# Attention and feed-forward on one core: values' products with tokens on partitions from the third block on, and one burst for values and the next scores in the main loop

## The chip, the cores and the metric

The kernel runs on one core of a Trainium2 chip. The metric is the device time of one execution in microseconds; 0.2% of it, 1.2 us, is about what a measurement of this kernel can tell from no change.

## The reference, cut to what matters

Local attention over chunks of 32 tokens (each chunk sees 8 memory keys, 16 tokens to its left, itself and 8 tokens to its right, so 64 keys), and on its result two large products with a smooth gate between them. Everything is float32.

```python
B, H, S, D = 4, 8, 768, 64                      # 3072 tokens, 24 chunks of 32 per sequence
for c in range(nc):                             # per chunk
    k_full = np.concatenate([mem_k, k_ctx], axis=2)      # 64 keys
    v_full = np.concatenate([mem_v, v_ctx], axis=2)
    scores = scale * np.matmul(q_c, k_full.transpose(0, 1, 3, 2))
    a = np.exp(scores - np.max(scores, axis=-1, keepdims=True))
    a = a / (np.sum(a, axis=-1, keepdims=True) + 1e-09)
    out[:, :, c_start:c_end] = np.matmul(a, v_full)      # "values' products"
x = out.transpose(0, 2, 1, 3).reshape(B * S, H * D)      # 3072 x 512
h = x @ w_in                                             # 512 x 2048
g = np.where(h >= 1, h, np.where(h <= -1, 0.0, (h + 1) ** 2 / 4))
return g @ w_out                                         # 2048 x 512
```

## The kernel before

The 3072 tokens are six blocks (NB) of 512. A block's attention is done in two halves of 256 tokens, a half being one key `(block, half)` in the code. The feed-forward of a block is 16 steps: step `s` makes 128 of the 2048 hidden features for all 512 tokens (`pe_hidden`, 12 matmuls of 128x128 by 512 into one PSUM bank of the pool `ps_h`, which has two), passes them through the gate on ScalarE and VectorE (`gating`, `gate_sum`, `gate_high`, `gate_low`), and multiplies them with `w_out` (`pe_out`, 12 matmuls into the block's accumulators `ps_o`). Twelve, since each float32 operand is split in a high and a low part of TensorE's faster type (`xth`/`xtl`, `gh`/`gl`, two parts of the weights `wr`), and three of the four products are made. LAG = 2: at step `s` TensorE does `pe_hidden(s)` and then `pe_out(s-2)`, so two steps pass between a hidden feature and its use.

A half's attention is a chain of stages. `pe_scores` makes 64 products of 32 query tokens with 64 keys into the two-bank PSUM tile "s"; the products are float32 and small, eight places of the array (64 rows by 32 columns) hold one each. Each is done by two instruction pairs, so a burst is 128 weight loads and 128 matmuls in the profile. `less_max` and `normalise` make the softmax on VectorE with the exponential on ScalarE; `transpose_prob` turns the probabilities on VectorE in 32x32 squares (six STREAM_TRANSPOSE, `pt<-pr`). `pe_values` takes the values as the stationary operand (64 keys by 64 features, four places of the array) and the turned probabilities as the moving one (32 tokens), so that the result has features on partitions, as `pe_hidden` wants x. It too is 64 products, 128 pairs, into the tile "s" again, now named `ps_x`. `x_high` (ScalarE) and `x_low` (VectorE) split that result into `xth` and `xtl`.

The order of the work is the program's: every engine call goes through the wrapper `InOrder`, whose line, 63, is the line of nearly all rows of the profile. The first third of the program is ordered by the hand-written string `FIRST` (blocks 0 and 1 of the feed-forward, attention of blocks 0 to 2; the names n2 and n3 in it are the halves of block 2). From there on the loop over `s` from step 32 to 95 sets it: blocks 2 to 5 of the feed-forward, and the attention of blocks 3 to 5, six halves, ahead of their use. `STARTS = (3, 9)` puts the scores of the halves at steps 3 and 9 of each of the three blocks before; the next three steps hold softmax, transposes and values, so that the values' burst comes three steps after the scores' (`begin.get(s - stage)`). In a step, TensorE's order is: scores or values burst if there is one, `pe_hidden(s)`, `pe_out(s-2)`. Each burst therefore stands by itself between the large matmuls. The loads of the next half (`load_qk`, 1.5 MB, and `load_v`, 1 MB, one buffer each) are issued by SyncE when the burst that used the buffer is done.

Of the kernel before, what the change touches and what calls it, by code (L numbers as in the profile page):

```python
# [8 lines left out]
F32 = mybir.dt.float32  # L9
# [13 lines left out]
LAG = 2  # L23


STARTS = (3, 9)

# [13 lines left out]
    w15 J13 J15 n1 J15 n1 J14 C0 J15 n1 J14 n1 n1 C0 n1 n1 J15 C1 n1 n1 J15 n1 C1 n1 n1 C1 C0 C1 C2  # L43
    J15 J15 C0 C1 n1 J15 J15 C0 C2 C2 C0 + n1 C2 n1 n1 C3 C2 C1 C3 C3 D0 C3 C3 C2 D0 D0 D1 D0 D0 n2
    D1 D1 D2 D1 + n2 C3 D1 D2 n2 D0 D2 n2 D2 D3 n2 D2 D1 n2 n2 D3 n2 E4 D3 n2 D3 n2 n2 n2 D2 E4 D3
    n2 E5 n2 E4 E4 E4 D3 E5 E6 E5 E5 E5 E4 E6 E6 E6 n2 E6 E7 + n2 n2 n2 n3 E7 E5 + n3 n3 E7 E8 n3 E7
    n3 n3 n3 E6 n3 E8 n3 n3 n3 E9 n3 n3 n3 E8 n3 E7 E8 E9 E8 E7 + n3 E9 E9 n3 n3 E9 E10 E8 E10 E10
    E10 E11 E10 E9 E11 E11 E11 E12 E11 E10 E12 E12 E12 E13 E12 E11 E13 E13 E13 E14 E13 E12 E14 E14
    E14 E15 E14 E13 E15 E15 E15 E15
"""  # L50

LAST = 2
# [16 lines left out]
def attn_ffn_kernel(ctx: ExitStack, tc: tile.TileContext, first_qk, first_v, qk, vw, w, out):  # L69
# [51 lines left out]
    def load_qk(blk, half):  # L121
        t = qk_of[blk, half] = apool.tile([P, NP, QKN], F32, name="qk", tag="qk")
        sp.dma_start(t, qk[blk - 1, half].rearrange("p (h f) -> p h f", h=NP))

    def load_v(blk, half):
        t = v_of[blk, half] = apool.tile([P, NP, VN], F32, name="v", tag="v")
        sp.dma_start(t, vw[blk - 1, half].rearrange("p (h f) -> p h f", h=NP))
# [40 lines left out]
        yield  # L168


    scores_of, prob, prob_t, banks, xts, both = {}, {}, {}, {}, {}, {}

    def x_of(blk):
        if blk not in xts:
# [113 lines left out]
    def pe_scores(key):  # L288
        src = qk_of.pop(key)
        ps = scores_of[key] = two_banks("s", "ps_s")  # L290
        s = ps.rearrange("p h (r t w) -> p h r t w", r=NP, w=W)
        for r in range(NP):
            for c in range(HC):
                t, j = divmod(c, P // CHUNK)
                for h in range(2):
                    rows, k0 = slice(h * D, (h + 1) * D), HT + c * W
                    pe.matmul(
                        s[j * CHUNK : (j + 1) * CHUNK, h, r, t],
                        src[rows, r, c * CHUNK : (c + 1) * CHUNK],
                        src[rows, r, k0 : k0 + W],  # L300
                        start=True,
                        stop=True,
                    )
# [24 lines left out]
    def pe_values(key):  # L328

        ps = banks[key] = two_banks("s", "ps_x")  # L330
        o = ps.rearrange("p a (r t b q) -> p a r t b q", r=NP, t=2, q=CHUNK)
        pt = prob_t.pop(key).rearrange("p b (h r t) q -> p b h r t q", h=2, r=NP)
        v = v_of.pop(key).rearrange("p r (t b h d) -> p r t b h d", t=2, b=2, h=2)
        for r in range(NP):
            for t in range(2):
                for b in range(2):
                    for a in range(2):
                        rows = slice(a * D, (a + 1) * D)
                        for h in range(2):
                            pe.matmul(  # L340
                                o[h * D : (h + 1) * D, a, r, t, b],
                                v[rows, r, t, b, h],
                                pt[rows, b, h, r, t],
                                start=True,
                                stop=True,
                            )
# [10 lines left out]
    def x_high(key):  # L357
        for a in range(2):
            src, hi, _ = x_views(key, a)
            act.copy(hi, src)  # L360

    def x_low(key):
        for a in range(2):
            src, hi, lo = x_views(key, a)
            dve.tensor_tensor(lo, src, hi.bitcast(F32), op=ALU.subtract)
            yield
        banks.pop(key)

    def attention(key):

        pe_scores(key)
        yield
        yield from less_max(key)
        act.activation(prob[key], prob[key], AF.Exp, scale=SCALE)
        yield
        yield from normalise(prob[key])
        yield from transpose_prob(key)
        pe_values(key)
        yield
        x_high(key)  # L380
        yield
        yield from x_low(key)

    def run(*chains):

# [174 lines left out]
        next(chains[name])  # L560


    begin = {}
    first = 2
    for blk in range(first + 1, NB):
        for half in range(2):
            begin[(blk - 1) * NFC + STARTS[half]] = (blk, half)

    def after(key):
        blk, half = key  # L570
        return (blk + half, 1 - half)

    steps = NB * NFC
    for s in range(first * NFC, steps):
        k_scores, k_probs, k_trans, k_values = (begin.get(s - stage) for stage in range(4))
        if k_scores is not None:
            pe_scores(k_scores)
            if after(k_scores)[0] < NB:
                load_qk(*after(k_scores))
        if k_values is not None:  # L580
            pe_values(k_values)
            x_high(k_values)
            if after(k_values)[0] < NB:
                load_v(*after(k_values))
        if s > first * NFC:
            gate_sum(s - 1)
            gate_high(s - 1)
        run(
            gate_low(s - 1) if s > first * NFC else None,
            x_low(k_values) if k_values is not None else None,  # L590
        )
        run(
            less_max(k_scores) if k_scores is not None else None,
            normalise(prob[k_probs]) if k_probs is not None else None,
            transpose_prob(k_trans) if k_trans is not None else None,
        )
        if k_scores is not None:
            act.activation(prob[k_scores], prob[k_scores], AF.Exp, scale=SCALE)
        pe_hidden(s)
        gating(s)  # L600
        if s - LAG >= first * NFC:
            pe_out(s - LAG)
            if (s - LAG) % NFC == NFC - 1:
                store((s - LAG) // NFC)
        else:
            n, i = LAST // LAG, s - first * NFC
            for name in items[len(items) - LAST :][i * n : (i + 1) * n]:
                for _ in chains[name]:
                    pass
    gate_sum(steps - 1)  # L610
    gate_high(steps - 1)
    run(gate_low(steps - 1))
# [16 lines left out]
def _lay_out(q, k, v, mem_k, mem_v, moe_w_in, moe_w_out):  # L629
    import numpy as _np  # L630

    B, H, S, D = q.shape
    NM, NC = mem_k.shape[2], S // CHUNK
    NP, W = H // 2, NM + LEFT + CHUNK + RIGHT
    NB = B * S // TB

    def windows(mem, a):

        pad = _np.pad(a, ((0, 0), (0, 0), (LEFT, RIGHT), (0, 0)))
        win = [  # L640
            _np.concatenate([mem, pad[:, :, c * CHUNK : (c + 1) * CHUNK + LEFT + RIGHT]], axis=2)
            for c in range(NC)
        ]
        return _np.stack(win, axis=1).reshape(B * NC, H, W, D)

    def transposed(a):

        return a.transpose(1, 3, 0, 2).reshape(NP, 2 * D, -1)


    qt = transposed(q).reshape(NP, 2 * D, NB * 2, TB // 2).transpose(2, 1, 0, 3)
    kw = windows(mem_k, k).reshape(NB * 2, NCH // 4, 2, NP, 2, 2, W // 2, D)

    k0 = kw.transpose(0, 4, 7, 3, 1, 2, 5, 6).reshape(NB * 2, 2 * D, NP, NCH // 2 * W)
    kw = _np.stack([kw[:, :, 0], kw[:, :, 1][..., ::-1, :, :]], axis=2)
    kw = kw.transpose(0, 4, 7, 3, 1, 2, 5, 6).reshape(NB * 2, 2 * D, NP, NCH // 2 * W)
    qk0 = _np.concatenate([qt, k0], axis=3)[0:2].reshape(2, 2 * D, 2, -1).transpose(0, 2, 1, 3)
    qk = _np.concatenate([qt, kw], axis=3).reshape(NB, 2, 2 * D, -1)[1:]
    vw = windows(mem_v, v).reshape(NB, NT, 4, NP, 2, W, D)

    v0 = vw[0].reshape(2, 2, 4, NP // 2, 2, 2, W, D).transpose(0, 3, 1, 6, 4, 2, 5, 7)

    v1 = vw[1:].reshape(NB - 1, 2, NT // 2, 2, 2, NP, 2, W, D).transpose(0, 1, 3, 7, 5, 2, 4, 6, 8)
    DM, DF = moe_w_in.shape
    n = DF // 128

    slices = (
        moe_w_in.reshape(DM // 128, 128, n, 128).transpose(2, 1, 0, 3).reshape(n, 128, DM),
        moe_w_out.reshape(n, 128, DM),
    )  # L670
    w = _np.stack([slices[which][fc] for which, fc in weight_order(n)])
    w = w.reshape(n, 2, 128, DM).transpose(0, 2, 1, 3).reshape(n, 128, 2 * DM)
    arrays = {

        "first_qk": qk0.reshape(NP, 2 * D, -1),
        "first_v": v0.reshape(NP, 2 * W, NCH * D),
        "qk": qk,
        "vw": v1.reshape(NB - 1, 2, 2 * W, -1),
        "w": _np.ascontiguousarray(w).view(_np.int64),
    }  # L680
    return {name: _np.ascontiguousarray(a) for name, a in arrays.items()}
# [23 lines left out]
```

## Time and profile before

| what | value |
|---|---|
| median of 3 runs | 600.14 us (599.96 to 600.18) |
| the profiled execution | 600.11 us |
| its span in the trace | 598.3 us |
| TensorE matmuls busy (PE) | 582.7 us, 97% |
| VectorE (DVE) / ScalarE (ACT) busy | 325.6 us, 54% / 280.3 us, 47% |
| chain that ended last | PE 82%, DVE 15%, issue 2%, DMA 1% |

The span is what the profiler sees of the program; 1.8 us of the execution lie outside it. The chain is the work that ended last, followed back from the end: it says which engine set the time at each moment. DVE's share of it lies in the first 107 us, where weights are decoded; from there to the last stores it consists of PE's matmuls alone.

### The profile page before, as it was taken

What the parts mean: (1) busy time and instruction counts of PE and PEld (TensorE: products, weight loads), DVE (VectorE), ACT (ScalarE), POOL (GpSimd) and SP (SyncE); (2) the same over time, 40 slices, a digit from 0 to 9 for tenths busy, and PEclk for the clock granted to TensorE, in tenths of its full rate; (3) what the DMA queues carried; (4) which work ended last, traced back from release to release, by engine and by line L of the source; (5) the groups of instructions that cost most, each with busy time, mean ns of one, the idle gap of its engine ahead of it and who ended that gap; (6) DMA issues with size and microseconds to landing.
All of it is one profiled execution on the core that took longest, in us unless ns stands there. A gap on an engine that the chain in (4) does not pass through costs nothing.

```text
span 598.3 us, 12265 instructions
## 1 busy us (share of the span) xinstructions
PE 582.7 (97%) x5496; PEld 483.5 (81%) x5496; DVE 325.6 (54%) x466; ACT 280.3 (47%) x503; POOL 0.7 (0%) x6
## 2 busy tenths in 40 slices
PE   5899999999999999999999999999999999999996
PEld 2888888788888888888888888888888888888885
DVE  5999999986474224636423644623564632322222
ACT  2689864554435335444435443434443444543442
POOL 0000000000000000000000000000000000000000
PEclk9999999999999999999999999999999999999999
DMA  8999300424051004012101223200310000100001
GB/s 355 422 418 419 148 1 0 178 82 168 1 177 71 0 1 158 26 65 108 71 1 71 107 71 107 71 1 34 144 71 2 1 2 0 71 0 1 0 1 70
DMA packets 9844, 55.31 MB, mean 92 GB/s; under 512 B 1088, under 2 KB 1088, under 8 KB 5184
## 3 DMA queue, kind: packets, MB, share of 16 engines
q1 hardware_dynamic: 9792, 54.53, 23.6%
q8 instruction: 43, 0.70, 0.5%
q14 instruction: 9, 0.07, 0.0%
HBM read 48.23 MB, written 6.29 MB: 91 GB/s over the span
## 4 chain that ended last, share of the span: by engine, by line
PE 82%; DVE 15%; issue 2%; DMA 1%; ACT 0%; DVEq 0%; ACTq 0%
PE ps_o L63 38%; PE ps_h L63 38%; DVE f L63 6%; PE ps_x L63 3%; DVE wr L63 2%; PE ps_s L63 2%; DVE gw L63 1%; DVE gl L63 1%; DVE pr L63 1%; DVE den L63 1%; DMA qk<-in_first_qk_dram 1%; DVE pt L63 1%; DVE mx L63 1%; DVE xtl L63 0%; DVE rin L63 0%
## 5 line engine op out<-in xcount | busy, mean ns | idle before, releaser
L63 PE MATMUL ps_h<-xth,wr 128*128 128x512 f32 (+1 forms) x832 | 195.6, 377 | 1.1 <-DVE wr L63 1.1
L63 PE MATMUL ps_o<-wr,gh 128*128 128x512 f32 x768 | 194.7, 390 | 0.0
L63 PEld LDWEIGHTS ps_h<-xth,wr 128*128 128x128 f32 x832 | 149.0, 190 | 30.3 <-DVE wr L63 1.5
L63 PEld LDWEIGHTS ps_o<-wr,gh 128*128 128x128 f32 x768 | 143.3, 188 | 29.4
L63 DVE SCALAR_TENSOR_TENSOR gw<-gw,gt 128x512 f32<-128x512 f32 (+1 forms) x104 | 67.2, 649 | 164.9 <-ACT gw L63 164.6
L63 ACT ACTIVATE gw<-ps_h 128x512 f32<-128x512 f32 (+1 forms) x104 | 58.6, 563 | 159.0 <-PE ps_h L63 158.9
L63 PE MATMUL ps_o<-wr,gl 128*128 128x512 f32 x384 | 106.9, 389 | 0.0
L63 PE MATMUL ps_h<-xtl,wr 128*128 128x512 f32 (+1 forms) x416 | 104.8, 374 | 0.0
L63 DVE TENSOR_TENSOR gl<-gw,gh 128x512 fp32r<-128x512 f32 (+1 forms) x104 | 67.4, 649 | 65.8 <-ACT gh L63 65.7
L63 ACT CAST gh<-gw 128x512 fp32r<-128x512 f32 (+1 forms) x104 | 61.1, 590 | 69.9 <-DVE gw L63 69.9
L63 PEld LDWEIGHTS ps_h<-xtl,wr 128*128 128x128 f32 x416 | 75.3, 190 | 13.9
L63 PEld LDWEIGHTS ps_o<-wr,gl 128*128 128x128 f32 x384 | 72.1, 188 | 15.1
L63 ACT ACTIVATE gw<-gw 128x512 f32<-128x512 f32 (+1 forms) x104 | 62.4, 600 | 0.0
L63 ACT ACTIVATE gt<-ps_h 128x512 f32<-128x512 f32 (+1 forms) x104 | 58.3, 561 | 0.0
L63 DVE STREAM_TRANSPOSE pt<-pr 32x512 f32<-32x512 f32 (+1 forms) x60 | 41.2, 698 | 1.3
L63 DVE SCALAR_TENSOR_TENSOR f<-w,f 128x1024 uint32<-128x1024 uint32 x32 | 39.0, 1220 | 0.4
L63 ACT ACTIVATE pr<-pr 128x1024 f32<-128x1024 f32 (+1 forms) x14 | 13.1, 937 | 35.1 <-DVE pr L63 35.0
L63 PEld LDWEIGHTS ps_x<-pt,v 64*64 64x64 f32 x1536 | 25.1, 142 | 5.0 <-issue 3.3
L63 PE MATMUL ps_x<-pt,v 64*64 64x32 f32 x1536 | 26.6, 226 | 1.2 <-ACT pt L63 1.2
L63 ACT CAST xth<-ps_x 128x512 fp32r<-128x512 f32 x24 | 13.1, 591 | 20.6 <-PE ps_x L63 20.6
L63 ACT CAST wr<-f 128x1024 fp32r<-128x1024 f32 x16 | 16.8, 1051 | 11.7 <-DVE f L63 11.7
L63 PEld LDWEIGHTS ps_s<-qk 64*32 64x32 f32 x1536 | 17.1, 112 | 6.1 <-issue 3.1
(27 smaller groups left out, 182.6 us busy)
## 6 DMA issues: line engine op xcount, KB each, us to landing
w<-in_w_dram SPq DMA_DIRECT2D x16, 1024.0 KB, 19.8
qk<-in_qk_dram SPq DMA_DIRECT2D x10, 1536.0 KB, 6.5
v<-in_vw_dram SPq DMA_DIRECT2D x10, 1024.0 KB, 5.5
out_dram<-ob SPq DMA_DIRECT2D x24, 256.0 KB, 2.0
qk<-in_first_qk_dram SPq DMA_DIRECT2D x4, 768.0 KB, 8.7
v<-in_first_v_dram SPq DMA_DIRECT2D x4, 512.0 KB, 12.7
```

What stands on the lines that cost most here:

```text
L63: return self.tc.keep_in_program_order(getattr(self.engine, name)(*args, **kwargs))
```

## The change

From block 2 on (`first = 2`) the values' products are made the other way round. `pe_rows` takes the turned probabilities as the stationary operand (64 keys by 32 tokens) and the values as the moving one (64 features), so that tokens are on partitions and the array holds eight products at a time; it is again 64 products, 128 pairs. Since `pe_hidden` needs features on partitions, the result must be turned: `rows_out` copies it from PSUM to the tile `xr` (two ScalarE copies), `turn_rows` turns it on VectorE in six STREAM_TRANSPOSE into the tile `xt`, `split_high` makes `xth` (one ScalarE cast) and `split_low` makes `xtl` (one VectorE subtraction). On the host the second half of each value row is rolled by 32 features, so that quarters of the partitions land where they should.

For the two halves of block 2 (n2 and n3 in `FIRST`) the result stays in the tile "s". In the main loop it goes to the two banks of `ps_h`, the pool of the hidden features, and the schedule changes: `BURSTS = (1, 6, 11, 19, 27, 35, 43)` are seven steps, counted from the loop's first. At the n-th of them the values of half n-1 and the scores of half n follow each other on TensorE without anything between; the first has scores only, the last values only. In a step with values, `pe_out(s-2)` now comes ahead of `pe_hidden(s)`. Softmax and transposes of a half follow its scores one, two and three steps later; the exponential comes behind the gate's three instructions on ScalarE instead of ahead of them. In `FIRST`, n3 starts some steps later than before, with its scores in the place behind n2's values that they had.

The core of the diff:

```diff
-STARTS = (3, 9)
+BURSTS = (1, 6, 11, 19, 27, 35, 43)
+    def pe_rows(key, outs):
+        banks[key] = outs
+        pt = prob_t.pop(key).rearrange("p b (h r t) q -> p b h r t q", h=2, r=NP)
+        v = v_of.pop(key).rearrange("p r (t b h d) -> p r t b h d", t=2, b=2, h=2)
+        for r in range(NP):
+            for t in range(2):
+                for b in range(2):
+                    for a in range(2):
+                        rows = slice(a * D, (a + 1) * D)
+                        for h in range(2):
+                            to, c0 = (2 * h + b) * CHUNK, (r * 2 + t) * D
+                            pe.matmul(
+                                outs[a][to : to + CHUNK, c0 : c0 + D],
+                                pt[rows, b, h, r, t],
+                                v[rows, r, t, b, h],
+                                start=True,
+                                stop=True,
+                            )
+    def rows_out(key):
+        xr = rows_of[key] = apool.tile([P, NP, 2, 2, D], F32, name="xr", tag="pt")
+        for a, src in enumerate(banks.pop(key)):
+            act.copy(xr[:, :, :, a], src.rearrange("p (r t d) -> p r t d", r=NP, t=2))
+    def turn_rows(key):
+        src = rows_of.pop(key).rearrange("p r t a (s q) -> p r (t a) s q", s=2)
+        xt = turned[key] = apool.tile([P, NP, HT], F32, name="xt", tag="pr")
+        dst = xt.rearrange("p r (n b q) -> p r n b q", b=2, q=CHUNK)
+        for b in range(2):
+            dve.transpose(dst[:, :, :, b], src[:, :, :, 0])
+            yield
+        for b in range(2):
+            for h in range(2):
+                of, to = (2 * h + b) * CHUNK, (2 * h + 1 - b) * CHUNK
+                dve.transpose(dst[to : to + CHUNK, :, :, b], src[of : of + CHUNK, :, :, 1])
+                yield
+    def split_high(key):
+        act.copy(x_half(x_of(key[0])[0], key[1]), turned[key])
+    def split_low(key):
+        hi, lo = (x_half(x, key[1]) for x in x_of(key[0]))
+        dve.tensor_tensor(lo, turned.pop(key), hi.bitcast(F32), op=ALU.subtract)
+        yield
...
+    for s in range(first * NFC, steps):
+        stages = [begin.get(s - stage, (None, None)) for stage in range(4)]
+        k_values, k_scores = stages[0]
+        if k_values is not None:
+            pe_rows(k_values, [ps_h.tile([P, 512], F32, name="ps_h") for _ in range(2)])
+            if after(k_values)[0] < NB:
+                load_v(*after(k_values))
+        if k_scores is not None:
+            pe_scores(k_scores)
+            if after(k_scores)[0] < NB:
+                load_qk(*after(k_scores))
+        if k_values is not None:
+            product(s)
+        if s > first * NFC:
+            gate_sum(s - 1)
+            gate_high(s - 1)
+        if k_values is not None:
+            rows_out(k_values)
+        split, k_max = stages[1]
+        run(
+            split_low(split) if split is not None else None,
+            gate_low(s - 1) if s > first * NFC else None,
+        )
...
+        pe_hidden(s)
+        gating(s)
+        if k_values is not None:
+            split_high(k_values)
+        if k_max is not None:
+            act.activation(prob[k_max], prob[k_max], AF.Exp, scale=SCALE)
+        if k_values is None:
+            product(s)
```

TensorE in the main loop, at the seventh step of block 2's feed-forward. Before, this is the values' burst of half (3, 0); `wr_721` and its neighbours are weight tiles, `ps_h<-xth,wr` a hidden group, `ps_o<-wr,gh` an output group, x8 and x4 are counts:

```order
L63 MATMUL ps_h<-xth,wr_721 128x512 x8
L63 MATMUL ps_h<-xtl,wr_721 128x512 x4
L63 MATMUL ps_o<-wr_721,gh 128x512 x8
L63 MATMUL ps_o<-wr_721,gl 128x512 x4
L63 MATMUL ps_x<-pt,v 64x32 x64
L63 MATMUL ps_h<-xth,wr_796 128x512 x8
L63 MATMUL ps_h<-xtl,wr_796 128x512 x4
L63 MATMUL ps_o<-wr_796,gh 128x512 x8
L63 MATMUL ps_o<-wr_796,gl 128x512 x4
```

The same place in the changed kernel, TensorE again:

```order
L63 MATMUL ps_h<-xth,wr_721 128x512 x8
L63 MATMUL ps_h<-xtl,wr_721 128x512 x4
L63 MATMUL ps_o<-wr_721,gh 128x512 x8
L63 MATMUL ps_o<-wr_721,gl 128x512 x4
L63 MATMUL ps_h<-v,pt 32x64 x64
L63 MATMUL ps_s<-qk 32x64 x64
L63 MATMUL ps_o<-wr_796,gh 128x512 x8
L63 MATMUL ps_o<-wr_796,gl 128x512 x4
L63 MATMUL ps_h<-xth,wr_796 128x512 x8
L63 MATMUL ps_h<-xtl,wr_796 128x512 x4
L63 MATMUL ps_h<-xth,wr_850 128x512 x8
L63 MATMUL ps_h<-xtl,wr_850 128x512 x4
```

The scores of the next half have moved up behind the values, the values are written by tiles of the scores' form, and the output group of this step stands ahead of its hidden group, so that two hidden groups follow each other.

VectorE around the same values' burst, before:

```order
L63 SCALAR_TENSOR_TENSOR gw<-gw,gt 128x512
L63 TENSOR_TENSOR gl<-gw,gh 128x512
L63 TENSOR_TENSOR xtl<-ps_x,xth 128x4x2x64 x2
L63 SCALAR_TENSOR_TENSOR gw<-gw,gt 128x512
L63 TENSOR_TENSOR gl<-gw,gh 128x512
```

VectorE around it in the changed kernel:

```order
L63 SCALAR_TENSOR_TENSOR gw<-gw,gt 128x512
L63 TENSOR_TENSOR gl<-gw,gh 128x512
L63 STREAM_TRANSPOSE xt<-xr 128x16x32 x2
L63 STREAM_TRANSPOSE xt<-xr 32x16x32 x4
L63 SCALAR_TENSOR_TENSOR gw<-gw,gt 128x512
L63 TENSOR_TENSOR xtl<-xt,xth 128x4x256
L63 TENSOR_TENSOR gl<-gw,gh 128x512
L63 MEMSET ps_s 32x8x8
L63 TENSOR_REDUCE mx<-ps_s 128x16
L63 TENSOR_TENSOR pr<-ps_s,mx 128x1024
```

Six transposes stand behind the gate of the step before, and the subtraction and the next half's softmax follow in the step after it.

ScalarE around the burst in the changed kernel (before, two casts `xth<-ps_x` stood ahead of a `gh<-gw`):

```order
L63 CAST gh<-gw 128x512
L63 COPY xr<-ps_h 128x8x64 x2
L63 ACTIVATE gw<-ps_h 128x512
L63 ACTIVATE gt<-ps_h 128x512
L63 ACTIVATE gw<-gw 128x512
L63 CAST xth<-xt 128x4x256
L63 CAST gh<-gw 128x512
```

The copies out of PSUM stand behind `gh` of the step before, and the cast to `xth` stands ahead of `gh` of the burst's own step.

## Rows read from the trace of the kernel before

**Rows 1.** Busy time in the main loop: us, then each engine, PEclk, DMA share, GB/s.

```profile
222.23:585.50 363.27, 363.27 (x3037) 300.25 (x3037) 155.61 (x224) 153.63 (x275) 0.00 (x0) 1.00 0.14 49
```

**Rows 2.** Chain that ended last, main loop: start us, us, what.

```profile
233.11 1.41 PE ps_s L63 x91
234.52 2.97 PE ps_h L63 x12
237.49 2.72 PE ps_o L63 x12
...
251.09 2.00 PE ps_x L63 x128
253.09 2.95 PE ps_h L63 x12
```

**Rows 3.** Timeline of PE, main loop: start us, us, instruction, count.

```profile
232.04 1.07 PE L63 MATMUL ps_o<-wr,gl 128*128 128x512 f32 x4
233.04 1.48 PE L63 MATMUL ps_s<-qk 64*32 64x64 f32 x128
234.45 2.12 PE L63 MATMUL ps_h<-xth,wr 128*128 128x512 f32 x8
236.41 1.08 PE L63 MATMUL ps_h<-xtl,wr 128*128 128x512 f32 x4
...
239.14 1.07 PE L63 MATMUL ps_o<-wr,gl 128*128 128x512 f32 x4
240.04 1.98 PE L63 MATMUL ps_h<-xth,wr 128*128 128x512 f32 x8
241.86 1.07 PE L63 MATMUL ps_h<-xtl,wr 128*128 128x512 f32 x4
...
251.02 2.07 PE L63 MATMUL ps_x<-pt,v 64*64 64x32 f32 x128
253.01 2.11 PE L63 MATMUL ps_h<-xth,wr 128*128 128x512 f32 x8
```

**Rows 4.** Groups by form, whole span: count, busy us, mean ns, idle before.

```profile
L63 PE MATMUL ps_x<-pt,v 64*64 64x32 f32 x1536 | 26.6, 226 | 1.2 <-ACT pt L63 1.2
L63 PE MATMUL ps_s<-qk 64*32 64x64 f32 x1536 | 19.6, 239 | 1.1 <-DMA qk<-in_first_qk_dram 1.1
```

**Rows 5.** The same chain at the halves of block 2 (n2, n3).

```profile
161.71 2.00 PE ps_x L63 x128
163.71 2.95 PE ps_h L63 x12
...
179.20 2.00 PE ps_x L63 x128
```

**Rows 6.** Waits of PEld from 160 us on: total us, times, longest.

```profile
PEld ps_x L63 <- issue: 2.8, 8, 0.4
PEld ps_s L63 <- issue: 2.5, 7, 0.4
```

**Rows 7.** Groups by form, VectorE and ScalarE, whole span.

```profile
L63 DVE STREAM_TRANSPOSE pt<-pr 32x512 f32<-32x512 f32 x40 | 28.1, 703 | 1.2
L63 DVE TENSOR_TENSOR wr<-f,wr 128x1024 fp32r<-128x1024 f32 x16 | 19.5, 1218 | 0.0
L63 ACT CAST wr<-f 128x1024 fp32r<-128x1024 f32 x16 | 16.8, 1051 | 11.7 <-DVE f L63 11.7
L63 DVE TENSOR_TENSOR xtl<-ps_x,xth 128x512 fp32r<-128x512 f32 x24 | 15.6, 684 | 3.0 <-ACT xth L63 3.0
L63 DVE STREAM_TRANSPOSE pt<-pr 128x512 f32<-128x512 f32 x20 | 13.1, 689 | 0.1
L63 ACT CAST xth<-ps_x 128x512 fp32r<-128x512 f32 x24 | 13.1, 591 | 20.6 <-PE ps_x L63 20.6
```

**Rows 8.** Timeline of DVE and ACT just ahead of a burst.

```profile
251.03 0.69 DVE L63 SCALAR_TENSOR_TENSOR gw<-gw,gt 128x512 f32<-128x512 f32 x1
...
248.90 0.59 ACT L63 ACTIVATE gt<-ps_h 128x512 f32<-128x512 f32 x1
249.38 0.63 ACT L63 ACTIVATE gw<-gw 128x512 f32<-128x512 f32 x1
```

**Rows 9.** DMA issues: count, KB each, median us to landing.

```profile
qk<-in_qk_dram SPq DMA_DIRECT2D x10, 1536.0 KB, 6.5
```

More of the change, by code (lines that the diff above doesn't have):

```diff
@@ L45 @@
     D1 D1 D2 D1 + n2 C3 D1 D2 n2 D0 D2 n2 D2 D3 n2 D2 D1 n2 n2 D3 n2 E4 D3 n2 D3 n2 n2 n2 D2 E4 D3
[L46 to L49, printed above, removed]
+    n2 E5 n2 E4 E4 E4 D3 E5 E6 E5 E5 E5 E4 E6 E6 E6 n2 E6 E7 + n2 n2 n2 E7 n3 E5 + n2 n2 E7 E8 E7 n2
+    E7 n2 E6 n2 E8 n2 n3 E8 E9 E8 n3 E8 E7 n3 E9 n3 E9 n3 n3 n3 E10 E9 E9 E8 E10 n3 n3 E10 n3 E11
+    E10 E10 n3 E9 E11 n3 n3 E11 E12 E11 E11 E10 n3 + E12 n3 E12 n3 n3 E13 E12 E12 n3 E11 E13 n3 n3
+    E13 E14 E13 E13 n3 E12 n3 E14 n3 E14 E15 E14 E14 E13 E15 E15 E15 E15
 """
@@ L168, in decode @@
         yield
-    scores_of, prob, prob_t, banks, xts, both = {}, {}, {}, {}, {}, {}
+    scores_of, prob, prob_t, banks, rows_of, turned, xts, both = {}, {}, {}, {}, {}, {}, {}, {}
+    first = 2
     def x_of(blk):
@@ L367, in x_low, with x_half @@
         banks.pop(key)
+    def pe_rows(key, outs):
[20 more added lines that the diff above has]
+            act.copy(xr[:, :, :, a], src.rearrange("p (r t d) -> p r t d", r=NP, t=2))
+    def x_half(x, half):
+        return x[:, :, half * HT : (half + 1) * HT]
+    def turn_rows(key):
[16 more added lines that the diff above has]
+        yield
     def attention(key):
@@ L377, in attention @@
         yield from transpose_prob(key)
-        pe_values(key)
+        if key[0] < first:
+            pe_values(key)
+            yield
+            x_high(key)
+            yield
+            yield from x_low(key)
+            return
+        ps = two_banks("s", "ps_x")
+        pe_rows(key, [ps[:, a] for a in range(2)])
         yield
-        x_high(key)
+        rows_out(key)
         yield
-        yield from x_low(key)
+        yield from turn_rows(key)
+        split_high(key)
+        yield
+        yield from split_low(key)
     def run(*chains):
@@ L560, in attn_ffn_kernel @@
         next(chains[name])
[L563 to L567, printed above, removed]
+    steps = NB * NFC
+    keys = [(blk, half) for blk in range(first + 1, NB) for half in range(2)]
+    begin = {first * NFC + at: (keys[n - 1] if n else None, keys[n] if n < len(keys) else None) for n, at in enumerate(BURSTS)}
     def after(key):
@@ L571, in after, with product @@
         return (blk + half, 1 - half)
[L573 to L600, printed above, removed]
+    def product(s):
         if s - LAG >= first * NFC:
@@ L609, in attn_ffn_kernel @@
                     pass
+    for s in range(first * NFC, steps):
[21 more added lines that the diff above has]
+        )
+        k_probs, k_trans = stages[2][1], stages[3][1]
+        run(
+            turn_rows(k_values) if k_values is not None else None,
+            less_max(k_max) if k_max is not None else None,
+            normalise(prob[k_probs]) if k_probs is not None else None,
+            transpose_prob(k_trans) if k_trans is not None else None,
+        )
+        pe_hidden(s)
[6 more added lines that the diff above has]
+            product(s)
     gate_sum(steps - 1)
@@ L661, in _lay_out @@
     v0 = vw[0].reshape(2, 2, 4, NP // 2, 2, 2, W, D).transpose(0, 3, 1, 6, 4, 2, 5, 7)
-    v1 = vw[1:].reshape(NB - 1, 2, NT // 2, 2, 2, NP, 2, W, D).transpose(0, 1, 3, 7, 5, 2, 4, 6, 8)
+    v1 = vw[1:].reshape(NB - 1, 2, NT // 2, 2, 2, NP, 2, W, D).transpose(0, 1, 3, 7, 5, 2, 4, 6, 8).copy()
+    v1[1:, :, :, :, :, :, 1] = _np.roll(v1[1:, :, :, :, :, :, 1], D // 2, axis=-1)
     DM, DF = moe_w_in.shape
```

## The prediction

> **What bounds the kernel now.** I read the busy table of the main loop first, then the chain that ended last, then TensorE's timeline around one burst of each kind. From the loop's start at 222.23 us to the end of its last steady step at 585.50 us TensorE is busy for all of 363.27 us, at a granted clock of 1.00 (its 2.4 GHz level), while VectorE is busy 155.61 and ScalarE 153.63 us [rows 1]. So this part is bound by TensorE alone; only what leaves TensorE's queue, or makes it wait, changes the time. From 160 us on the matmuls wait for nobody, and the weight loads show one idle gap of 0.4 us at most per burst, put down to issue, ahead of a change of tile form [rows 6].
>
> The chain prices a burst. A group of twelve large matmuls takes 2.72 us; a scores burst inserts 1.41 and makes the next group 2.97, a values burst inserts 2.00 and makes it 2.95 [rows 2]. Scores cost 1.41 + 0.25 = 1.66 us, values 2.00 + 0.23 = 2.23 us.
>
> The timeline splits these prices in work and a change of form. Ahead of the scores, four matmuls take 233.04 - 232.04 = 1.00 us, undisturbed 240.04 - 239.14 = 0.90: 0.10 lost. Behind them, eight take 236.41 - 234.45 = 1.96 against 241.86 - 240.04 = 1.82: 0.14 lost [rows 3]. The 128 small matmuls span 1.48 us with the last one's 0.24, so first start to last start is 1.24; the next large one starts 1.41 after the first small one, another 0.17 [rows 3, 4]. A change of form there and back costs 0.10 + 0.17 + 0.14 = 0.41, the scores themselves 1.24 (sum 1.65, as above). For the values 2.07 - 0.23 = 1.84 is work, and 2.23 - 1.84 = 0.39 change of form [rows 2 to 4]. I use 0.40, 1.25 and 1.84. The main loop has six bursts of each kind: 12 x 0.40 + 6 x 1.25 + 6 x 1.84 = 23.3 us on the path.
>
> **The change part by part.** *New form of the values.* The trace has no such burst, but the scores are one in every size that I can see: 128 pairs, stationary 64x32, moving 64 wide, eight places of the array, two PSUM banks. Only the order differs: scores alternate between the two row halves of the array at each product, the new burst does two products on one half and then two on the other, as the old values do. Bounds: at worst no better than the values, 1.84; at best each place turns round as fast as one of the values' places, which gives 1.84 x 4 / 8 = 0.92 with eight in use. The scores' 1.25 lies between and has the same form, so I take 1.25: 0.59 saved per burst. There are eight such bursts, six in the loop and two at n2 and n3, where TensorE is the chain as well and a burst costs the same 2.00 [rows 5]. 8 x 0.59 = 4.7 us.
>
> The Trainium skill speaks against this in "TensorE: Matmul & The Clock Gate", section "The mechanism" of its part on packing small matmuls: a weight load overlaps matmuls in flight only when it goes to another row group. The new order visits a row group twice running, and by that rule would gain less than the scores' rate suggests; that result is the second case below. The same page, in "Wait — 56ns, not 53.3ns?", gives a floor of about 25 ns from start to start of a matmul however small; 128 of them would take 3.2 us in either form, and here the trace disagrees, with 1.48 us for 128 [rows 3].
>
> *One burst for two.* The loop had twelve bursts, now seven. Each joint burst saves one change of form if small matmuls of one form follow each other freely. Bounds for the seam: 0, and a whole 0.40. Form, sizes and clock are the same on both sides, and inside a burst 128 of them run without a change of form, so it is nearer to 0; I take 0.05. Saved: 5 x 0.35 = 1.8 us.
>
> *Work for other engines.* Per half VectorE gets 2 x 0.689 + 4 x 0.703 = 4.19 us of transposes and one subtraction over 1024 columns (as the weights' one, 1.22) for two of 0.684: 4.0 us more. ScalarE gets two copies of 0.59 and one cast of 1.05 in place of two casts of 0.59: 1.05 more [rows 7]. Times six halves, in the loop VectorE goes from 156 to 180 and ScalarE from 154 to 160 of some 358 us. On the path this is nothing as long as TensorE is not made to wait, so I walk through a burst step with T the start of the values' products:
> - The rows need both banks of `ps_h`. The last hidden group ended at T - 2.72 and ScalarE has read its bank at T - 1.6 (249.49 against a burst at 251.09) [rows 2, 8]. Free.
> - The values' products end near T + 1.4. Ahead of the copies on ScalarE stands `gh` of the step before, behind a VectorE sum of 0.69 that can start at T - 1.0 when VectorE isn't in the transposes of a half (before, the sum came at 251.03 since it was) [rows 8]. The copies run from T + 1.4 to T + 2.6. The next hidden group, which wants the first bank, starts at T + 0.1 + 2 x 1.25 + 0.3 + 2.72 = T + 5.6, since the output group now stands ahead. 3 us of cover; had the hidden group stayed first, it would start at T + 2.9 and have 0.9.
> - VectorE turns from T + 2.7 to T + 6.9. ScalarE passes the hidden group that ended at T + 8.3 through the gate until T + 9.9, then casts to `xth` until T + 11.0. VectorE subtracts until T + 12.2, then makes `gl` of this step until T + 13.3. Its output group, with two hidden groups and one other output group ahead of it, starts at T + 16.5. Cover 3 us.
> - VectorE's softmax of 2.4 us follows, and ScalarE's exponential waits for it to T + 15.5, with the next step's `gh` queued behind it until T + 17.2; `gl` follows at T + 18 and is wanted at T + 22. Cover 4 us.
> - n3 is later than it was: from its products to block 2's first hidden group lie three hidden and three output groups, 16.3 us, against copies, transposes, cast, subtraction and the gates between them, some 11 us. Cover 5 us.
> - SyncE issues the next `v` and `qk` behind the products that free them, five steps (27 us) or more ahead of use, against 6.5 us to landing [rows 9]. Its waits hold up nothing else but stores.
>
> So none of it costs. Sum: 600.11 (profiled, span 598.3) - 4.7 - 1.8 = 593.6. The median stands 0.03 above the profiled execution: **593.6 us**.
>
> **The rivals.** *A, forecast: new values at the scores' rate, seam nearly free*, 593.6. For it: the same form; TensorE never idle. With the bounds of the rate (8 x 0.33 faster, or part of the way to 1.84) and of the seam (5 x 0.35 more) it reaches from 591.0 to 596.5.
>
> *B, the order, not the form, sets the rate*: two loads running on one row half make the new burst as long as the old values, 1.84. Only the changes of form are saved, 600.1 - 5 x 0.35 = 598.3. For it: the old values have that order and run at 1.84. Against it: their 128 pairs use four places and the scores' use eight, and 1.84 to 1.25 is explained by that.
>
> *C, slower: the turning is late*. The new transposes write every second group of 32 columns, which no row shows; the old ones read so and wrote in one piece. If the six took D instead of 4.2 us, the cast to `xth` would wait in ScalarE's queue with `gh` of the step behind it. The cover is used up when D passes 7.2 + 3.2 = 10.4 us, 1.7 us per transpose. At 2.1 us each, D = 12.6, TensorE waits 2.2 us in six steps, 13 us less the 6.5 gained: 607. Against it: the rows of two shapes agree at 0.69 and 0.70, 2.4 times below the point.
>
> *D, no difference*: the rate as in B and the seam dear, 600.1. For it stands only the idle gap of 0.4 at each burst's weight loads [rows 6], if it belongs to a burst's first wait and not to the change of form.
>
> **How the numbers follow.** A 0.85, B 0.07, C 0.04, D 0.04. The range leaves out C, D and the far end of B, and the fastest tip of A: 591.6 to 597.2, a little beyond A's slow end for rates on the way to B's. Differences within 0.2% (1.2 us) can't be told from none by a measurement of this kernel. Faster: A and B, 0.92. Same: D, 0.04. Slower: C, 0.04.
>
> **What would show it.** In the profile after: bursts `ps_h<-v,pt` of form 64*32 with 128 pairs in about 1.5 us, `ps_s` starting within 0.1 us of the last of them, and the next output group at 2.6 to 2.8 us from the first. `ps_x` in the old form only for blocks 0 and 1. Matmuls of TensorE still without waits from 160 us on. STREAM_TRANSPOSE `xt<-xr`, 48 of them, at 0.7 us each; VectorE busy near 358 us. It would be wrong if the new bursts take 2 us (B), if the next output group starts 3.1 us or more from the first (seam), or if a hidden group waits for ScalarE's copies or an output group for `gl` (C).

## The result and the profile after

The changed kernel is slower: 607.14 us (median; 605.62 to 609.25) against 600.11 for the kernel before (599.96 to 600.18). The ratio is 1.012, interval 1.0089 to 1.0151. The forecast of 593.6 was wrong by 13.5 us, more than half of it on the other side of "no change". The profiled execution is the slowest of the four, 609.25 us with a span of 607.5; its parts are summed against that number.

Two lines of the page of the kernel after: the busy times, and the instruction traffic (packets, MB, share of the DMA engines).

```profile
PE 581.7 (96%) x5496; PEld 482.0 (79%) x5496; DVE 356.8 (59%) x506; ACT 286.5 (47%) x511; POOL 0.7 (0%) x6
...
q8 instruction: 43, 0.70, 0.5%
```

VectorE has the forecast work (356.8, forecast 358). TensorE is busy for 1 us less than before, and the span is 9 us longer: so TensorE stands still somewhere. The chain of work that ended last says where. Here are the five joint bursts, as [rows 2] shows single ones, then the last burst, which has values only (start us, us, what):

```profile
249.96 1.41 PE ps_h L63 x91
252.37 1.76 issue
254.57 4.54 PE ps_o L63 x12
...
286.12 2.04 issue
288.57 4.54 PE ps_o L63 x12
...
335.79 2.13 issue
338.99 2.97 PE ps_o L63 x12
...
385.34 2.11 issue
387.87 4.54 PE ps_o L63 x12
...
435.06 1.59 issue
437.74 2.97 PE ps_o L63 x12
...
481.50 1.41 PE ps_h L63 x91
482.92 2.97 PE ps_o L63 x12
```

Two things are new against [rows 2]. In each joint burst stand 1.6 to 2.1 us of "issue", time in which TensorE waited for nothing that the profile shows. And three of the five output groups behind them take 4.54 us, where the other two and the one behind the last burst take 2.97. The values' burst itself takes 1.41 us instead of the 2.00 of [rows 2], as forecast.

TensorE's timeline in the first joint burst shows the place of the gap (start us, us, instruction, count, wait):

```profile
249.89 1.48 PE L63 MATMUL ps_h<-v,pt 64*32 64x64 f32 x128
251.17 1.19 PE L63 MATMUL ps_s<-qk 64*32 64x64 f32 x101
254.13 0.44 PE L63 MATMUL ps_s<-qk 64*32 64x64 f32 x27 [1.76 <-issue]
254.50 3.06 PE L63 MATMUL ps_o<-wr,gh 128*128 128x512 f32 x8
```

The scores start 251.17 - 249.89 = 1.28 us after the first values product, 0.03 more than the work of 1.25: the seam between the two kinds costs next to nothing here. The gap lies inside the scores, between the 101st matmul and the 102nd, which have the same form and read the same tile. In the third joint burst it stands earlier, behind some 42 of them (two lie in rows ahead of these):

```profile
335.15 0.64 PE L63 MATMUL ps_s<-qk 64*32 64x64 f32 x40
337.92 1.08 PE L63 MATMUL ps_s<-qk 64*32 64x64 f32 x86 [2.13 <-issue]
```

A cost that belonged to the change from values to scores would stand at one place. This one has the mark of a count. The windows from one gap's end to the next give it: behind the window stand its length, then busy time and number of instructions of PE, PEld, VectorE and ScalarE.

```profile
254.13:288.15 34.02, 31.98 (x382) 26.29 (x382) 21.54 (x30) 13.67 (x24) 0.00 (x0) 0.95 0.24 84
288.15:337.92 49.77, 47.64 (x384) 39.13 (x385) 26.57 (x40) 21.19 (x38) 0.00 (x0) 0.97 0.20 70
337.92:387.44 49.52, 47.42 (x511) 39.34 (x510) 26.27 (x38) 20.30 (x36) 0.00 (x0) 1.00 0.17 61
387.44:436.64 49.20, 47.61 (x383) 39.10 (x384) 25.71 (x37) 21.29 (x38) 0.00 (x0) 0.97 0.18 64
```

Matmuls and weight loads together are 764, 769, 1021 and 767: within a few records of 3, 3, 4 and 3 times 256. The few come from the edges of the windows and from semaphore waits, which stand in TensorE's queue too: counted with these from the program's start, the gaps stand at instructions 5826, 6594, 7361, 8386 and 9153, which are 768, 767, 1025 and 767 apart, multiples of 256 within one. The page's 43 instruction packets carry 0.70 MB, 16 KB each, and TensorE's 2 x 5496 instructions divided by 43 are about 256. So TensorE's program comes in pieces of 256 instructions, and all the gaps end at the same place of a piece. What the clock does behind them shows in the granted clock of two windows, around the output group of the first burst and around that of the third (the number after POOL's):

```profile
254.50:259.00 4.50, 4.50 (x21) 3.56 (x14) 2.16 (x4) 0.00 (x0) 0.00 (x0) 0.62 0.96 347
338.90:341.90 3.00, 3.00 (x22) 2.46 (x14) 1.77 (x3) 0.00 (x0) 0.00 (x0) 1.00 0.82 255
```

Behind the first gap the mean is 0.62, between the levels of 1.2 and 2.4 GHz, and the group costs 4.54 - 2.97 = 1.57 us more; behind the third it is 1.00.

### The profile page after: what moved, and what is told of

Its sections match the earlier page's. It is cut to its first block, busy times and chain, and to the rows that moved or that the text cites. A ratio compares the mean times of both kernels' runs of the same rounds, so it can differ in the third digit from the quotient of the medians.

```text
span 607.5 us, 12327 instructions
## 1 busy us (share of the span) xinstructions
PE 581.7 (96%) x5496; PEld 482.0 (79%) x5496; DVE 356.8 (59%) x506; ACT 286.5 (47%) x511; POOL 0.7 (0%) x6
## 4 chain that ended last, share of the span: by engine, by line
PE 80%; DVE 14%; issue 4%; DMA 1%; ACT 0%; DVEq 0%; ACTq 0%
PE ps_o L63 39%; PE ps_h L63 38%; DVE f L63 6%; PE ps_s L63 2%; DVE wr L63 2%; DVE gw L63 1%; DVE gl L63 1%; PE ps_x L63 1%; DVE pr L63 1%; DVE den L63 1%; DMA qk<-in_first_qk_dram 1%; DVE pt L63 1%; DVE mx L63 1%; DVE xtl L63 0%; DVE rin L63 0%
## 5 line engine op out<-in xcount | busy, mean ns | idle before, releaser
L63 PE MATMUL ps_o<-wr,gh 128*128 128x512 f32 x768 | 198.4, 396 | 0.0
L63 PE MATMUL ps_o<-wr,gl 128*128 128x512 f32 x384 | 109.0, 396 | 0.0
L63 PEld LDWEIGHTS ps_o<-wr,gl 128*128 128x128 f32 x384 | 73.8, 192 | 15.7
L63 DVE STREAM_TRANSPOSE xt<-xr 32x512 f32<-32x512 f32 (+1 forms) x48 | 32.9, 699 | 13.9 <-ACT xr L63 13.3
L63 PE MATMUL ps_s<-qk 64*32 64x64 f32 x1536 | 20.4, 236 | 10.8 <-issue 9.6
L63 PEld LDWEIGHTS ps_s<-qk 64*32 64x32 f32 x1536 | 17.2, 110 | 14.8 <-issue 11.8
L63 ACT CAST wr<-f 128x1024 fp32r<-128x1024 f32 x16 | 16.8, 1050 | 11.8 <-DVE f L63 11.7
L63 DVE COPY ob<-ps_o 128x512 f32<-128x512 f32 (+1 forms) x16 | 9.6, 622 | 20.5 <-PE ps_o L63 20.5
```

The lines of the kernel that those rows point to most:

```text
L63: return self.tc.keep_in_program_order(getattr(self.engine, name)(*args, **kwargs))
```

## The experiments

The theory tested is called **supply**: the next piece of TensorE's program is fetched only when TensorE has passed the end of an earlier one, and comes some 3.3 us later. The 256 instructions of one burst (128 loads, 128 matmuls) are used up in 1.25 us, so whoever passes two ends within small products stands still until the piece is there. One burst has 256 instructions and passes one end; a joint burst has 512 and passes two. In the trace the second burst's gap fits: by the instructions' count an end is passed at 284.59, one packet of 16 KB runs on the instruction queue within 285.3 to 286.9 and none from 284.6 to 285.3, and TensorE goes on at 288.15, 3.6 us after the end. The rivals are the **seam** (a change of product kind or of target inside a burst costs some 2 us), **contention** (the loads of the next `v` and `qk`, issued together, delay something) and the **new form** of the values.

**The output group between the two bursts.** Same work, only TensorE's order and what follows from it differs:

```diff
             if after(k_values)[0] < NB:
                 load_v(*after(k_values))
+            product(s)
         if k_scores is not None:
             pe_scores(k_scores)
...
-        if k_values is not None:
-            product(s)
```

> The changed kernel with the output group of the burst's step put between values and scores of the joint burst (order on TensorE: values, twelve large matmuls, scores, hidden group); nothing else differs. Supply theory: TensorE's instructions arrive in pieces of 256, and a piece is asked for only when TensorE passes the end of the one before; it came 3.1 to 3.7 us later in the changed kernel, while 256 instructions of small products are used up in 1.3 us. With 2.7 us of large matmuls (24 instructions) between the bursts no stall is left, TensorE's clock stays at 1.00, twelve changes of form are paid, and only the new form saves: 600.1 - 8 x 0.59 = 595.4 us (594.8 to 596.5). Seam theory (a wait or a change at the first score holds TensorE about 2 us whatever stands ahead): five stalls of about 2 us stay, 605 us or more.

Measured: 595.14 us (595.11 to 595.20) against 599.87 before in the same session, ratio 0.9922 (0.9905 to 0.9938). TensorE's matmuls have no wait at all from 165 us on, and the clock of the main loop is 1.00. The chain at the first burst:

```profile
249.71 1.41 PE ps_h L63 x91
251.12 2.95 PE ps_o L63 x12
254.07 1.41 PE ps_s L63 x91
```

One group of twelve large matmuls, 2.95 us, between the two bursts removes all the gaps and all the clock falls, 12 us. It is faster than both kernels; the version that follows can't be told from it.

**The new form alone.** The kernel before, with `pe_rows` and the turning from block 2 on, but its own schedule (`STARTS = (3, 9)`, single bursts), and with the changed kernel's order in `FIRST`:

```diff
         if k_values is not None:
-            pe_values(k_values)
-            x_high(k_values)
+            ps = two_banks("s", "ps_x")
+            pe_rows(k_values, [ps[:, a] for a in range(2)])
...
+        if k_values is not None:
+            rows_out(k_values)
...
         run(
+            turn_rows(k_values) if k_values is not None else None,
             less_max(k_scores) if k_scores is not None else None,
```

> The new form of the values alone, with the schedule of before in the main loop (scores at steps 3 and 9, values three steps later, into the tile of the scores; copies, transposes and split follow them), the new string for the first third. Supply theory: no burst is longer than 256 instructions, no stall, clock 1.00, 600.1 - 8 x 0.59 = 595.4 us (594.8 to 596.5). If instead the new form has a price of its own that the joint burst hid, it shows here: above 597.

Measured: 595.30 us (595.12 to 596.53), ratio 0.9928 (0.9914 to 0.9943), no waits of the matmuls from 165 us on. The new form brings the 4.7 us that it was forecast to bring (599.87 - 595.30 = 4.6), and isn't what made the kernel slower.

**Joint bursts with the old form.** The changed kernel, but in the main loop the values are made by the kernel before's products (features on partitions, `x_high` and `x_low`, no turning), into the two banks of `ps_h`:

```diff
-            pe_rows(k_values, [ps_h.tile([P, 512], F32, name="ps_h") for _ in range(2)])
+            pe_old(k_values, [ps_h.tile([P, 512], F32, name="ps_h") for _ in range(2)])
```

> The joint bursts alone: in the main loop the changed schedule, but the values' products in the old form (four places of the array, features on partitions, no turning); the two halves of block 2 keep the new form. Supply theory: each joint burst has 512 instructions as before and stalls; since the old values are slower the 256 between two ends take 1.4 to 1.7 us, so stalls are 1.7 to 2.0 us instead of 2.0 to 2.4. 600.0 - 1.2 (new form twice) - 0 to 1.8 (changes of form saved) + 5 x 1.9 = 606.5 to 608.3 us, 1.6 more for each fall of the clock. If the stall needed the new form: 597 to 599.

Measured: 606.06 us (605.74 to 607.61), ratio 1.01 (1.0084 to 1.0117). The waits of the matmuls (us, times, longest), and the chain at the first joint burst:

```profile
PE ps_s L63 <- issue: 6.8, 5, 1.9
```

```profile
249.80 2.00 PE ps_h L63 x128
251.80 1.13 PE ps_s L63 x74
252.93 1.89 issue
```

The five gaps are there without the new form. They are shorter in sum, 6.8 against 9.6 us, which fits: the old values take 2.00 us, so more of the fetch lies under work. They are also shorter than expected, 0.9 to 1.9 us each instead of 1.7 to 2.0, and the time lies 0.4 us under the expected range. This takes the two halves of the change apart: the form gains 4.6 us. The joint burst loses 7.3 with the old form (606.06 against 599.95 before in that session, which the new form of block 2's two halves lowers by some 1.2) and 11.8 with the new one (607.14 against 595.30).

**A burst of 512 without any seam.** The kernel before, in which each scores burst of the main loop makes the same 64 products twice (the second time over the first; the result is the same):

```diff
-        for r in range(NP):
+        for r in [r for _ in range(times) for r in range(NP)]:
...
-            pe_scores(k_scores)
+            pe_scores(k_scores, 2)
```

> The kernel before, with the scores of each main-loop half made twice running into the same place (6 x 128 more small pairs, no new wait, no new tile, no values beside them, no load issued ahead of them). Supply theory: each of these bursts now has 512 instructions, so it passes two ends of a piece within 1.3 us and stalls some 1.8 to 2.4 us in its second half, at places 256 instructions (or a multiple) apart; 600.1 + 6 x 1.25 + 6 x 2.1 = 620 us, more where the clock falls after a stall (1.6 us each). Seam theory: the second pass is like the first, no stall, 600.1 + 6 x 1.25 = 607.6 us. Contention theory (the load of the next values, issued in the middle of the joint burst, slows the fetch): no such load here, so no stall or a much shorter one, below 610 us.

Measured: 620.5 us (one run). The timeline of TensorE in the first such burst, all the waits of the matmuls, and the instruction traffic:

```profile
233.20 1.96 PE L63 MATMUL ps_s<-qk 64*32 64x64 f32 x174
236.96 1.04 PE L63 MATMUL ps_s<-qk 64*32 64x64 f32 x82 [1.81 <-issue]
...
PE ps_s L63 <- issue: 11.3, 6, 2.1
...
q8 instruction: 49, 0.80, 0.5%
```

One kind of product, one target, the loads of before, and the same gaps: six in six bursts. The 6 x 256 added instructions are six more packets on the instruction queue, 49 for 43. Around the first gap, from 234.5 to 237.2 us, the trace shows one packet on all DMA queues together, and it is the instruction packet: no load runs there. Neither seam nor contention nor the new form can be the cause of these. The excess of 20.6 us is 6 x 1.25 = 7.5 for the added products and 11.3 of waits, and 1.8 more around them. The clock stayed at 1.00 behind all six.

**Half of the scores behind the values.** The first 64 pairs of the scores directly behind the values, then the output group, then the other 64, so that a burst has 384 instructions:

```diff
+        for r in range(NP):
+            if r == NP // 2:
+                yield
...
+            parts_s = pe_scores_parts(k_scores)
+            next(parts_s)
...
         if k_values is not None:
             product(s)
+            if k_scores is not None:
+                for _ in parts_s:
+                    pass
```

> The changed kernel with only the first half of the scores (64 pairs) behind the values; the output group follows, then the other half of the scores, then the hidden group. A joint burst has 384 instructions. Supply theory, from the places of the ends of pieces in the changed kernel's TensorE queue (counted 203, 215, 85, 211 and 81 instructions into the five joint bursts): only in the third and the fifth does a second end (341 and 337 instructions in) fall inside the 384, so those two stall 1.8 to 2.4 us and the other three don't stall at all. Time: 12 changes of form as before, 600.1 - 4.7 + 2 x 2.1 = 599.6 us, up to 603 if the clock falls. Seam theory: all five stall, about 606 us.

Measured: 599.97 us (one run). From the chain, the first burst, the third, and the gap of the fifth:

```profile
249.89 1.41 PE ps_h L63 x91
251.30 0.65 PE ps_s L63 x41
251.95 2.97 PE ps_o L63 x12
...
328.72 0.42 PE ps_s L63 x26
329.15 1.88 issue
...
425.08 1.94 issue
```

Only the third and the fifth have a gap, the two that the count of instructions had named: 384 instructions hold two ends of a piece or one, depending on where the burst begins. The bursts are alike in all else.

**The same, moved by 128 instructions.** The kernel just shown, with 64 tiny matmuls more at the start of the program, which nothing reads; they are 128 instructions on TensorE:

```diff
+        for _ in range(64):
+            pe.matmul(ps[:, 0:32], warm[:, 0:P], warm[:, 0:32], start=True, stop=True)
```

> The half-joint kernel of before (values, first half of the scores, output group, second half of the scores) with 64 tiny matmuls more at the very start of the program, where TensorE waits for its first data: 128 instructions, and nothing else, so every later instruction stands 128 places further on. Supply theory: the ends of the pieces of 256 now fall 75, 87, 213, 83 and 209 instructions into the five joint bursts, the second ones 331, 343, 469, 339 and 465: stalls of about 2.1 us move to the first, second and fourth joint burst, and the third and fifth, which stalled, run through. Time 600.0 + 2.1 = 602.1 us, up to 1 more for the start, 1.6 more for each fall of the clock. Any theory by which the data, the waits or the neighbours of the bursts make the stall: third and fifth stall as they did, 600.0 to 601.

Measured: 606.24 us (one run). The chain: an extra gap in the first third of the program, then the first to fifth burst of the main loop.

```profile
169.68 0.90 PE ps_o L63 x3
170.58 0.87 issue
...
254.91 1.86 issue
...
287.57 1.53 issue
...
335.73 0.62 PE ps_s L63 x38
...
383.02 1.86 issue
385.31 4.54 PE ps_o L63 x12
...
433.09 0.62 PE ps_s L63 x38
```

The gaps moved from the third and fifth burst to the first, second and fourth, as expected, though the added instructions run at the very start of the program. Counted from there, they stand at instructions 5826, 6594 and 8386, exactly where the first, second and fourth gap of the changed kernel stand: the bursts have moved, the ends of the pieces have not. The time is 4.1 us over what was expected. Against the 599.97 us of the kernel just shown it is 6.3 more, and four things make 6.1 of these: three gaps in place of two (5.2 against 3.8 us), n2's values 2.2 us later (163.91 against 161.73 in the chain; why is open), the slow clock behind the fourth burst (1.6), and a gap of 0.87 us, which no other kernel has, in the output group behind n3's scores. That last one matters for single bursts: n2's values and n3's scores have a whole hidden group of 2.95 us between them. But one end falls on the first few of n3's scores and the next, 256 instructions on, three large matmuls behind the last, so that a single burst of 256 nearly fills a piece and TensorE runs dry just behind it.

**How much work must lie between.** The output group's first 4, and its first 8, of 12 matmuls between the bursts, the rest behind the scores:

```diff
-            product(s)
+            rest = pe_out_parts(s - LAG, 4)
+            next(rest)
         if k_scores is not None:
             pe_scores(k_scores)
...
+        if k_values is not None:
+            for _ in rest:
+                pass
```

> The changed kernel with only the first four of the output group's twelve matmuls between values and scores, the other eight behind the scores. Supply theory: the 256 instructions between two ends now take 0.26 + 0.91 + 0.41 (change of form) + 0.95 = 2.5 us instead of 1.3; a piece comes 3.2 to 3.6 us after it was asked for, so each of the five stalls shrinks to 0.7 to 1.1 us. 595.2 + 5 x 0.9 = 599.7 us (598.5 to 601). A stall that belongs to the seam would be gone, as it is with twelve between them, and the time 595.2.

> The changed kernel with eight of the output group's twelve matmuls between values and scores, four behind the scores. Supply theory: with four between, a piece came 3.15 to 3.65 us after it was asked for and 0.6 to 1.15 us of stall were left; eight add 0.91 us between the two ends, so stalls of 0 to 0.25 us are left: 595.2 to 596.4 us, clock at 1.00 in the main loop.

Measured: 599.63 and 595.77 us (one run each). With 4 the waits of the matmuls (us, times, longest) are

```profile
PE ps_s L63 <- issue: 3.4, 5, 0.9
```

and with 8 there are none. The four matmuls last about 1.0 us, and the longest gap shrinks by about as much, from 2.1 to 0.9; eight last 2.0 and cover it. The five gaps with 4 are 0.4 to 0.9 us, a little less than the 0.7 to 1.1 expected. What decides is the time between two ends of a piece, not whether the bursts touch.

**The changed kernel again**, unchanged, beside these:

> The changed kernel again, to see what of its time changes from execution to execution. Theory: the five stalls are there each time (10 to 11 us in all); what differs is how many of them are followed by a stretch at half clock, 0 to 5 at 1.6 us each. Times of about 604.2 plus a multiple of 1.6: 604 to 610 us. In the kernel with the group between (no stalls) the four times lay within 0.1 us.

Measured: 607.71 us (606.52 to 608.94), ratio 1.013 (1.0113 to 1.0147). The waits of the matmuls, and the first burst's output group:

```profile
PE ps_s L63 <- issue: 9.1, 5, 2.1
```

```profile
254.51 4.54 PE ps_o L63 x12
```

Five gaps again, in sum a little less than the 10 to 11 us expected, and slow groups behind the first, third and fourth of them, where it was the first, second and fourth in the profile shown above. The gaps belong to the program; the falls of the clock vary from one execution to the next. That fits the spread of the changed kernel's times, 3.6 us (605.62 to 609.25), where those of the kernel before spread over 0.2.

The Trainium skill, "Runtime: NRT & Kernel Launch", section "Instruction fetch mechanics", describes blocks of 16 KiB, 256 instructions, refilled in order, and calls the cost of crossing one "mostly hidden". On the size of a block the trace agrees (43 packets, 0.70 MB, gaps at multiples of 256 apart); on the cost it disagrees here, with 9.6 us in five bursts. No number above rests on the page.

## Why the prediction was wrong, point by point

**The new form at the scores' rate: right.** Taken 1.25 us of work, 8 x 0.59 = 4.7 saved. On the chain the burst takes 1.41 as the scores' does, and the form alone gave 4.6. Rival B, where the order sets the rate, fell: it asked for 2.00 on the chain.

**The seam: right in itself, but the bound failed, and with it the sum.** The step put the price of joining the bursts between 0 and 0.40 us, "inside a burst 128 of them run without a change of form". The seam is 0.03 us in the first joint burst. But the row it leaned on shows 256 instructions, and it was stretched to 512 as though TensorE's queue were always full. The price of joining is not at the joint: it is the second end of a piece, 1.6 to 2.1 us of waiting at each of five bursts, four to five times the upper bound. It is the walk's condition, "as long as TensorE is not made to wait", that broke: the walk asked it of engines and loads, and not of TensorE's own program. The "issue" of [rows 6] is not this wait, and the prediction read it rightly as the change of form: the kernel with the new form alone, which has no gap, shows the same 2.8 and 2.5 us there. No gap over 0.4 stands in the trace of before, so this size could not be read from it, but nor was there a row with more than 256 small instructions in a run that could carry an upper end of 0.40.

The sum with the measured terms: from the first values product to the next output group the forecast was 2.6 to 2.8 us, in the middle 2.7. In the five bursts it is 4.61 (254.50 - 249.89 in the first), 4.96, 5.04, 5.11 and 4.50, together 24.2, so 10.7 more than 5 x 2.7; 9.6 of it are the gaps. Three groups at the slow clock, for which the forecast had no term, add 3 x 1.57 = 4.7. With these, 593.6 becomes 593.6 + 10.7 + 4.7 = 609.0, against 609.25 of the profiled execution.

**The change of form saved, 5 x 0.35 = 1.8: not got.** The two versions without gaps, with single bursts (595.30) and with only a group between (595.14), pay all the changes of form, and both are where the new form alone puts the kernel, 600.1 - 4.7 = 595.4. The 1.8 us would need bursts that touch, and bursts of 512 instructions that touch had a gap in every case.

**Work for other engines costs nothing: right.** ScalarE and VectorE around the first joint burst of the kernel after (start us, us, engine, instruction, wait):

```profile
251.41 1.07 ACT L63 COPY xr<-ps_h 128x512 f32<-128x512 f32 x2 [1.15 <-PE ps_h L63]
252.52 4.19 DVE L63 STREAM_TRANSPOSE xt<-xr 128x512 f32<-128x512 f32 x6 [1.53 <-ACT xr L63]
```

With T = 249.89 the copies start at T + 1.5 and the six transposes at T + 2.6 for 4.19 us, each within 0.2 us of the walk. The transposes, cast and subtraction that the rows of before could not show at these shapes:

```profile
L63 DVE STREAM_TRANSPOSE xt<-xr x48: 668/702/715, 164.3 to 487.5; 32x512 f32<-32x512 f32 x32, 128x512 f32<-128x512 f32 x16
L63 ACT CAST xth<-xt x8: 1048/1048/1053, 170.7 to 490.1; 128x1024 fp32r<-128x1024 f32 x8
L63 DVE TENSOR_TENSOR xtl<-xt,xth x8: 1225/1226/1226, 171.8 to 491.2; 128x1024 fp32r<-128x1024 f32 x8
```

In ns (least, median, most), 702, 1048 and 1226 against 703, 1051 and 1218 taken from [rows 7]. Rival C, the late turning at 2.1 us per transpose, had the right time (607) by a mechanism that isn't there: no matmul waits for ScalarE or VectorE. Rival D made the seam dear by the idle gap of 0.4 at the weight loads; that gap belongs to the change of form, as said, and isn't what cost the time.

**The range.** It was built from bounds of the two prices that the prediction knew, so it was as narrow as they are. The missing case was a resource that no wait of the trace of before names: the program itself, fetched at some 3.3 us per 256 instructions, against 5.4 us that a step of 24 large matmuls (48 instructions) takes and 1.25 us for 256 small ones.

## What to carry to other kernels

Before putting bursts of small products side by side on TensorE, count their instructions: here 256 in 1.25 us ran at full rate and 512 stood still for about 2 us; 1.0 us of large matmuls between the two halves left gaps of up to 0.9, 2.0 us left none. One burst of 256 is no safe size either: where an end of a piece fell on its first few instructions, 0.87 us were lost just behind it. A gap that the profile puts down to issue and that breaks a run of equal instructions at different places in different bursts should be counted in instructions from gap to gap; equal remainders point to the program's supply. Then a change early in the program moves the gaps, so a version must be read at its own alignment.

## What the runs showed of the hardware

- From passing the end of a piece to going on, TensorE needed 3.0 to 3.7 us (after: 250.88 to 254.13, 284.59 to 288.15, 334.30 to 337.92, 383.72 to 387.44, 433.57 to 436.64, the ends placed by counting instructions). The fetch's packets start 0.7 to 1.0 us behind the end, and TensorE goes on 1.3 to 1.6 us after the last has landed. In the kernel after, 43 ends counted so stand against 43 packets. From 160 us on, at ends among large matmuls the packet starts ahead of the end, by 4.1 to 5.0 us, and at the end that closes a gap 1.1 to 2.3 us behind it. So what asks for a piece runs ahead of the matmuls where these are long, and an end there costs nothing; how far ahead it reads, no run measured by itself.
- Between pieces there is one in reserve and no more, as far as these runs show: every burst of 512 small-product instructions in the main loop has its gap, 21 of 21 (five in each of two profiles of the changed kernel, five with the old form, six with the scores doubled), and no burst of 256 in the main loop has one. Outside it there is the one of 0.87 us behind n3's scores in the moved kernel.
- A gap of 0.9 to 2.1 us inside small products was followed by the clock's lower level (1.2 GHz) in some cases: behind 3 of 5 in each profile of the kernel after, 1 of 5 with the old form, 1 of 3 in the moved kernel, 0 of 2 in the half-joint one, 0 of 6 with the scores doubled; behind the five gaps of 0.4 to 0.9 us with four matmuls between, never. Mostly it costs 1.57 us (4.54 against 2.97); the third burst of the second profile lost 1.3 (4.27) and the old form's third 1.1 (4.02 against 2.95). Why some and not others stays open; no run separated it.
